# A three-stage transformer block on one core: its planner gets one place per step, a rule for products and reads that share a double PSUM tile, longer v loads and fillers of 256 columns

## The chip, the cores and the metric

The kernel runs on one core of a Trainium2 chip. The metric is the device time of one execution in microseconds (us). Three runs of the kernel before gave 773.05, 774.28 and 776.44 us; their median, 774.28 us, is the time that is compared.

## The reference

Everything is computed from float32 attention inputs and 64-bit weights:

```python
# attention: q, k, v are (4, 8, 576, 64); heads 0-3 a plain window of 32, heads 4-7 a dilated one (32 keys, step 4)
scores = scale * np.matmul(q, k.transpose(0, 1, 3, 2))
scores = np.where(masks[None, :, :, :], scores, -1000000000.0)
attn = np.exp(scores - max); attn = attn / (sum + 1e-09)
x = np.matmul(attn, v)                            # then (2304, 512)
# gated layer: w_gate, w_val (512, 1536), w_out (1536, 512)
x = (silu(x @ w_gate) * (x @ w_val)) @ w_out
# second layer: w_in (512, 1024), w_out (1024, 512), g_ln (1024)
h = x @ w_in
solu = h * softmax(h)
out = (solu - mean) / np.sqrt(var + 1e-06) * g_ln @ w_out
```

## The kernel before, in words

All large products run in float16 with every operand split into a high and a low part, so that each product is three matmuls (`PASSES`, line 65: high by high, high by low, low by high). The weights come as 64-bit numbers; they are converted on the chip by integer and float operations on ScalarE (ACT), VectorE (DVE) and GpSimd (POOL) (`w_conv`, `w_scale`, `w_split`, lines 598 to 797), and q, k, v, the attention output x, the gated product u and y are split in the same way (`split`, line 512: a high part, then a low part of the difference).

The work goes through 4 batches and 12 blocks of 192 tokens. For each batch, four pairs of heads go through `prep_T` (line 993, q and k transposed by TensorE (PE) for batches 0 and 1, by DMA for 2 and 3), `s1` (1108, scores and exponentials), `s2` (1216, the turned probabilities) and `s3` (1262, product with v and the split of x, lines 1307 to 1313). For each block, six chunks of `a_chunk` (1318) give the gated product: 48 matmuls at line 1339, then a Silu on ACT at line 1351 and the gate on DVE at line 1360, here called gate 1, gate 2 and so on in their order on DVE. Then come `b_part` (1413, product with w_out at line 1423, result y, split into `yhl`), and for each 128 tokens `c_part`, `c_exp`, `c_post` (1460 to 1555, product at line 1471 and the softmax and normalisation), `z_T` (1561) and `d_part` (1589, the last product at line 1599 and the store).

PSUM is held in five tiles (line 297): `ps0`, `ps1`, `ps2` are double (two banks of 512 columns each), `ps3` is single, `ps4` holds sums in its first half and receives the fillers. Results of kind 2 (A chunks, scores, turned tiles, h) take a whole double tile. Results of kind 1 (x in `s3`, y in `b_part`, the output in `d_part`; line 313) take `ps3` or one half of a double tile.

The order of all of this is not that of the code. Each piece of work is a step with an engine, an assumed cost, and the data that it reads and writes (`Plan.step`, line 95). `Plan.schedule` (157) then goes through a modelled time and takes, of the steps that could start soonest on an engine, the one with the smallest `urg`. Before, `urg` is the TensorE time planned so far less a lead and less a number of its own for each part of the work (the table `sl` in `OPT`, line 61). The order that comes out is what every engine's queue executes; the real waits are semaphores, which keep the data right whatever the plan assumed. While the planned PE would wait, the plan inserts fillers (line 302, matmuls of a 128 by 128 tile of ones into the unused part of `ps4`), each planned at `FILL` (line 79), only for planned times below 320 us (`OPT["fill"]`), and with no waiting of their own in the plan. Loads go out from the SyncE queue (SP), except that two of the first four v loads are issued from ACT's queue (`vact`, line 55; `load`, line 835).

Of the kernel before, what the change touches and what calls it, by code (L numbers as in the profile page):

```python
# [27 lines left out]
    "alap": 0.0,  # L28
# [26 lines left out]
    "vact": [0, 0, 1, 1],  # L55
# [11 lines left out]

class Bank:


    def __init__(self, of, kind):
        self.of, self.kind, self.at, self.users = of, kind, None, 0

    def get(self):
        return self.of(self.at)

FILL = 128 / 2400 + 0.0027


class Plan:

    PIPE = {"ACT": 0.1, "DVE": 0.09, "PE": 0.16, "POOL": 0.05, "SP": 0.0}
    LAT = 0.05

    def __init__(self):
# [3 lines left out]
    def step(self, eng, cost, fn, r=(), w=(), lat=0.0, tab=None, dense=1.0, starts=1, port=False):  # L95
        deps = {}
        for k in r:
            if k in self.writer:
                d = self.writer[k]
                deps[d["n"]] = d  # L100
        for k in w:
            for d in self.readers.get(k, ()):
                deps[d["n"]] = d
            if k in self.writer:
                d = self.writer[k]
                deps[d["n"]] = d
        st = {"n": len(self.steps), "eng": eng, "cost": cost, "fn": fn, "deps": list(deps.values()), "lat": lat,
              "tab": tab, "dense": dense, "starts": starts, "port": port or eng == "POOL", "end": None, "left": len(deps), "outs": [], "part": self.part, "urg": self.urgency - self.lead - OPT["sl"].get(self.part, 0.0), "ready": 0.0}
        for d in st["deps"]:
            d["outs"].append(st)  # L110
        for k in w:
            self.writer[k], self.readers[k] = st, []
        for k in r:
            self.readers.setdefault(k, []).append(st)
        st["banks"] = {k for k in list(r) + list(w) if isinstance(k, Bank)}
        for k in st["banks"]:
            k.users += 1
        if eng == "PE":
            self.urgency += cost
        self.steps.append(st)  # L120
# [19 lines left out]
    def lags(self, t):  # L140
# [3 lines left out]
        return self.busy < OPT["keep"] * (into + 3.413) - 0.3  # L144

    def rank(self):

        f = OPT["alap"]
        for st in reversed(self.steps):
            late = st["urg"] + st["cost"] if st["eng"] == "PE" or not st["outs"] else 1e9  # L150
            for o in st["outs"]:
                late = min(late, o["rank"] - (self.LAT + st["lat"]) * f)
            st["rank"] = late - st["cost"] * (1.0 if st["eng"] == "PE" else f)
        for st in self.steps:
            st["urg"] = st["rank"]

    def schedule(self):
        if OPT["alap"]:
            self.rank()
        free, tab = {"SP": 1.9, "ACT": 1.9, "DVE": 0.6, "POOL": 0.6}, "exp"  # L160
        self.busy, self.warm, self.window = 0.0, False, 0
        ready = [st for st in self.steps if not st["left"]]

        bank_free, order, issued, done = [0.0] * 8, [], 0.6, []
        held = {"DVE": [], "POOL": []}
        choices = {2: [(0, 1), (2, 3), (4, 5)], 1: [(6,), (0,), (1,), (2,), (3,), (4,), (5,)], "sum": [(7,)]}
        no = float("inf")

        def places(kind):

            for at in choices[kind]:
                broken = 0 if kind != 1 or at[0] == 6 else bank_free[at[0] ^ 1] != no
                yield max(bank_free[x] for x in at), broken, at

        while ready:
            cand, soonest = [], {kind: min(places(kind))[0] for kind in choices}
            for st in ready:
                t = max(free.get(st["eng"], 0.0), st["ready"])
                if st["port"]:
                    for a, b in held["POOL" if st["eng"] == "DVE" else "DVE"]:  # L180
                        if a <= t < b:
                            t = b
                for k in st["banks"]:
                    if k.at is None:
                        t = max(t, soonest[k.kind])
                if t == no:
                    continue

                on = st["eng"] == "POOL" and st["ready"] <= free["POOL"] == t
                cand.append((t, not on, st["urg"], st["n"], st))  # L190
# [65 lines left out]
def kernel(  # L256
# [13 lines left out]
    nc = tc.nc  # L270
# [29 lines left out]
    def idle(n):  # L300
        for _ in range(n):
            nc.tensor.matmul(out=ps_t[4][:, 0, 256:384], lhsT=ones, rhs=ones, start=True, stop=True)  # L302
# [1584 lines left out]
```

## Time and profile before

| | |
|---|---|
| median of three runs | 774.28 us |
| the profiled execution: its own time | 775.11 us |
| the profiled execution: its span | 773.3 us |
| PE busy | 742.7 us, 96% of the span |
| DVE, ACT, POOL busy | 510.3, 474.7, 233.0 us |
| fillers | 781 matmuls, 52.4 us busy |
| mean granted PE clock | 0.993 of full speed |

The span runs from the first to the last instruction that the profiler saw; the execution's own time holds 1.8 us more, around the span. A busy time is the union of an engine's instructions. The clock is the share of 2.4 GHz that was granted to PE, so that 0.5 is its lower level, 1.2 GHz.

### The profile page before, as it was taken

What the parts mean: (1) busy time and instruction counts of PE and PEld (TensorE: products, weight loads), DVE (VectorE), ACT (ScalarE), POOL (GpSimd) and SP (SyncE); (2) the same over time, 40 slices, a digit from 0 to 9 for tenths busy, and PEclk for the clock granted to TensorE, in tenths of its full rate; (3) what the DMA queues carried; (4) which work ended last, traced back from release to release, by engine and by line L of the source; (5) the groups of instructions that cost most, each with busy time, mean ns of one, the idle gap of its engine ahead of it and who ended that gap; (6) DMA issues with size and microseconds to landing.
All of it is one profiled execution on the core that took longest, in us unless ns stands there. A gap on an engine that the chain in (4) does not pass through costs nothing.

```text
span 773.3 us, 19396 instructions
## 1 busy us (share of the span) xinstructions
PE 742.7 (96%) x8044; PEld 622.2 (80%) x8044; DVE 510.3 (66%) x1059; ACT 474.7 (61%) x1020; POOL 233.0 (30%) x188
## 2 busy tenths in 40 slices
PE   6998999989999999999999999989999999999998
PEld 6888989889996888668865889968867889897754
DVE  3688988988987969778795557556665133116653
ACT  2878988976665767878762457656744344426432
POOL 1445145574663233142452124423420000110000
PEclk9999999999999999999999999999999999999999
DMA  8885933423435242645845371434222101001101
GB/s 205 212 260 180 247 125 109 112 72 110 148 70 160 60 113 50 131 106 90 144 105 112 76 118 20 77 79 77 44 45 44 26 15 29 14 3 21 35 14 55
DMA packets 149816, 71.79 MB, mean 93 GB/s; under 512 B 136032, under 2 KB 136032, under 8 KB 149216
## 3 DMA queue, kind: packets, MB, share of 16 engines
q1 hardware_dynamic: 146688, 69.80, 37.2%
q8 instruction: 63, 1.03, 0.6%
q10 hardware_dynamic: 3040, 0.75, 0.6%
q14 instruction: 25, 0.20, 0.1%
HBM read 46.14 MB, written 4.72 MB: 66 GB/s over the span
## 4 chain that ended last, share of the span: by engine, by line
PE 78%; DVE 10%; ACT 7%; DMA 3%; SPq 2%; issue 1%; ACTq 0%; DVEq 0%
PE ps L1339 28%; PE ps L1423 18%; PE ps L1471 12%; PE ps L1599 12%; PE ps L302 3%; PE ps L1152 2%; ACT sm L1193 1%; DMA area<-in_moe_w_gate_dram 1%; PE ps L1280 1%; SPq L857 1%; DVE sml L1174 1%; PE ps L1237 1%; PE ps L1275 1%; SPq L838 1%; DVE area L641 1%
## 5 line engine op out<-in xcount | busy, mean ns | idle before, releaser
L1339 PE MATMUL ps<-x,gv 128*128 128x192 f16 x3456 | 296.6, 247 | 3.3 <-DVE area L1360 2.3
L1339 PEld LDWEIGHTS <-gv 128*128 128x128 f16 x3456 | 286.7, 98 | 10.9 <-issue 5.3
L1423 PE MATMUL ps<-uhl,area 128*128 128x192 f16 x1728 | 150.1, 246 | 2.8 <-DVE x L531 1.9
L1423 PEld LDWEIGHTS <-area 128*128 128x128 f16 x1728 | 142.3, 98 | 6.0 <-issue 3.3
L1471 PE MATMUL ps<-area,yhl 128*128 128x512 f16 x432 | 98.7, 381 | 0.0
L1599 PE MATMUL ps<-area 128*128 128x512 f16 x408 | 94.0, 383 | 3.0 <-DVE yhl L531 3.0
L1360 DVE SCALAR_TENSOR_TENSOR u<-ps,c_gv,si 128x384 f32<-128x384 f32 x60 | 36.4, 611 | 77.2 <-ACT si L1351 77.2
L1212 POOL TENSOR_TENSOR sm<-sm,sml 96x768 f32<-96x768 f32 x28 | 46.5, 1662 | 118.4 <-DVE sml L1208 76.0
L1471 PEld LDWEIGHTS <-yhl 128*128 128x128 f16 x432 | 41.2, 98 | 46.2 <-issue 1.1
L1599 PEld LDWEIGHTS <-area 128*128 128x128 f16 x408 | 39.2, 98 | 47.4 <-issue 4.4
L1351 ACT ACTIVATE si<-ps,c_gv 128x384 f32<-128x384 f32 x72 | 41.4, 578 | 46.9 <-PE ps L1339 42.2
L1531 POOL TENSOR_TENSOR sml<-sml,nhalf 128x2 f32<-128x2 f32 x18 | 13.4, 743 | 167.3 <-DVE sml L1528 161.0
L302 PE MATMUL ps<-ones 128*128 128x128 bf16 x781 | 52.4, 226 | 5.6 <-DVE wsc L485 3.8
L302 PEld LDWEIGHTS <-ones 128*128 128x128 bf16 x781 | 48.3, 102 | 6.8 <-issue 4.5
L611 POOL TENSOR_TENSOR area<-area 128x512 int32<-128x512 int32 x28 | 38.4, 1388 | 47.4 <-ACT area L624 22.3
L1366 ACT ACTIVATE si<-u 128x384 f32<-128x384 f32 x60 | 31.2, 521 | 25.2 <-DVE u L1360 24.9
L543 POOL TENSOR_TENSOR qk<-qk,qk 96x768 f16<-96x768 f32 x16 | 27.8, 1735 | 47.0 <-DVE qk L522 25.7
L1193 ACT ACTIVATE sm<-sm,sml 96x128 f32<-96x128 f32 x96 | 37.2, 388 | 4.2 <-DVE sml L1187 3.9
L1496 ACT ACTIVATE area<-ps,sml 128x1024 f32<-128x1024 f32 x18 | 21.7, 1204 | 25.3 <-DVE sml L1491 25.1
L1551 ACT ACTIVATE area<-area,sml 128x1024 f32<-128x1024 f32 x17 | 21.0, 1237 | 22.8 <-DVE sml L1545 22.8
L1351 ACT ACT_TABLE_LOAD x24 | 30.8, 1283 | 4.6 <-PE ps L1339 4.2
L1490 DVE TENSOR_REDUCE sml<-ps 128x1 f32<-128x1024 f32 x18 | 21.9, 1218 | 17.5 <-PE ps L1471 15.5
(226 smaller groups left out, 1143.5 us busy)
## 6 DMA issues: line engine op xcount, KB each, us to landing
area<-in_moe_w_out_dram SPq DMA_DIRECT2D x10, 1024.0 KB, 4.9
area<-in_moe_w_gate_dram SPq DMA_DIRECT2D x6, 1024.0 KB, 7.5
area<-in_moe_w_val_dram SPq DMA_DIRECT2D x6, 1024.0 KB, 7.3
out_dram<-area SPq DMA_DIRECT2D x18, 256.0 KB, 2.0
area<-in_moe_w_in_dram SPq DMA_DIRECT2D x4, 1024.0 KB, 5.3
qk<-in_v_dram SPq DMA_DIRECT2D x9, 384.0 KB, 4.3
qk<-in_q_dram SPq DMA_DIRECT2D x20, 144.0 KB, 3.5
qk<-in_k_dram SPq DMA_DIRECT2D x18, 144.0 KB, 3.4
```

The costliest lines, as they stand in the source:

```text
L302: nc.tensor.matmul(out=ps_t[4][:, 0, 256:384], lhsT=ones, rhs=ones, start=True, stop=True)
L543: step("POOL", n / 480 + 0.05, lambda: nc.gpsimd.tensor_tensor(out=lo(), in0=src(), in1=hi(), op=ALU.subtract), r=list(sk) + list(hk), w=lk)
L611: step("POOL", 1.23, lambda: nc.gpsimd.tensor_tensor(out=ti[:, x], in0=ti[:, x], in1=part[:, x], op=ALU.add), r=rk, w=tk)
L1193: nc.scalar.activation(out=smv[:, n], in_=view()[0:QB, n // 3, n % 3] if on_pe else smv[:, n], func=ACTF.Exp, bias=nm[:, n:n + 1], scale=c ...
L1212: step("DVE" if OPT["pn"][b] else "POOL", dve(768) if OPT["pn"][b] else 1.43, lambda: on.tensor_tensor(out=smv, in0=smv, in1=rs.unsqueeze( ...
L1339: nc.tensor.matmul(out=view()[:, ff, w], lhsT=wt[:, a, kk, (f % 4) * 128:(f % 4) * 128 + 128], rhs=x[:, c, kk, BLK * o:BLK * o + BLK], sta ...
L1351: step("ACT", act(384) + 0.06, lambda: nc.scalar.activation(out=si, in_=view()[:, :, 0], func=ACTF.Silu, scale=c_gv[:, b, 2 * ci:2 * ci + 1]),
L1360: nc.vector.scalar_tensor_tensor(out=uu, in0=view()[:, :, 1], scalar=c_gv[:, b, 2 * ci + 1:2 * ci + 2], in1=si, op0=ALU.mult, op1=ALU.mult)
L1366: step("ACT", act(384) + 0.1, lambda: nc.scalar.activation(out=si.rearrange("p f t -> p (f t)"), in_=uu.rearrange("p f t -> p (f t)"), fun ...
L1423: nc.tensor.matmul(out=bk.get()[:, 0, cc * BLK:cc * BLK + BLK], lhsT=whl[6 + f // 4][:, a, f % 4, c * 128:(c + 1) * 128], rhs=uhl[:, e, f] ...
L1471: nc.tensor.matmul(out=bk.get()[:, half], lhsT=yhl[:, i, c, o:o + 128], rhs=w_in_hl[m][:, e, c % 2, half * 512:half * 512 + 512], start=(c ...
L1599: nc.tensor.matmul(out=bk.get()[:, 0], lhsT=zt[:, c, kk], rhs=whl[11 + half][:, e, kk % 4], start=(kk == 0 and n == 0), stop=(kk == 7 and ...
```

## The change

Five things change. The table `sl` and the function `rank` go; a list `PRI` holds one number for each step of the program, and `schedule` puts it into `urg`. The planner keeps for each bank when its neighbour in the double tile was last read and written (`beside`): a planned PE write of kind 1 doesn't start before the end of the reads of the other half, and a planned read not before the end of the writes to the other half. Assumed costs are raised: v loads to 2.5 or 3.9 us (from 2.05), `cgv`, `u_scale`, the plain `prep_T` copy and the split of x by 0.05 to 0.26 us. No v load is issued from ACT any more. A filler has 256 columns, on the same 128 weights. No other instruction's work is changed; a place in PSUM, and where a tile load or activation table falls, follows from the order.

```diff
-    "alap": 0.0,
-    "vact": [0, 0, 1, 1],
+    "vact": [0, 0, 0, 0],
-    "sl": {"A0.0": 705.2, "A0.1": 389.6,
...
+PRI = [
...
-FILL = 128 / 2400 + 0.0027
+FILL = 256 / 2400 + 0.0027
...
     def schedule(self):
-        if OPT["alap"]:
-            self.rank()
+        assert len(PRI) == len(self.steps)
+        for st, at in zip(self.steps, PRI):
+            st["urg"] = at
...
+        beside = {"read": [0.0] * 8, "written": [0.0] * 8}
...
-                yield max(bank_free[x] for x in at), broken, at
+                yield max([bank_free[x] for x in at] + ([beside["read"][at[0] ^ 1]] if kind == 1 and at[0] < 6 else [])), broken, at
...
                     if k.at is None:
                         t = max(t, soonest[k.kind])
+                    elif len(k.at) == 1 and k.at[0] < 6:
+                        t = max(t, beside["read" if st["eng"] == "PE" else "written"][k.at[0] ^ 1])
...
+                seen = beside["written" if st["eng"] == "PE" else "read"]
+                for x in k.at:
+                    seen[x] = max(seen[x], st["end"] + self.PIPE[st["eng"]] + self.LAT)
...
-            nc.tensor.matmul(out=ps_t[4][:, 0, 256:384], lhsT=ones, rhs=ones, start=True, stop=True)
+            nc.tensor.matmul(out=ps_t[4][:, 0, 256:512], lhsT=ones, rhs=ones.unsqueeze(1).to_broadcast([128, 2, 128]), start=True, stop=True)
...
-        step("DVE", 0.14, fn, r=[("wsc", 2 * c), ("wsc", 2 * c + 1), ("vsc", b)], w=[("cgv", b, c)])
+        step("DVE", 0.23, fn, r=[("wsc", 2 * c), ("wsc", 2 * c + 1), ("vsc", b)], w=[("cgv", b, c)])
...
-        load(2.05, fns, key, act=b == 0 and OPT["vact"][O0.index(pr)])
+        load(2.5 if dil else 3.9, fns, key, act=b == 0 and OPT["vact"][O0.index(pr)])
```

The program's lines move down by 90 from line 157 on: line 302 before is line 392 now, line 1360 is 1450. Counted over the whole program, the fillers go from 781 to 299, the loads of an activation table on ACT from 49 to 39, and everything else that PE, DVE and POOL execute stays in kind and number. Three places show how the order moves.

The head of SP's queue, which issues the loads (in a row: what is written, what is read, and x2 for two alike). Before:

```order
L595 DMA area_72<-in_moe_w_gate_dram 128x4x256
L838 DMA v32_1_91<-in_v_dram 96x2x64
...
L838 DMA v32_1_91<-in_v_dram 128x2x64
L838 DMA qk0_92<-in_q_dram 96x6x64 x2
L838 DMA uhl_109<-in_k_dram 96x6x64 x2
L595 DMA area_72<-in_moe_w_val_dram 128x4x256
L838 DMA yhl_110<-in_v_dram 96x2x64
```

And now:

```order
L928 DMA uhl_109<-in_k_dram 96x6x64 x2
L928 DMA qk0_92<-in_q_dram 96x6x64 x2
L685 DMA area_72<-in_moe_w_gate_dram 128x4x256
L928 DMA qk1_93<-in_q_dram 96x6x64 x2
L928 DMA v32_1_91<-in_v_dram 96x2x64
...
L928 DMA v32_1_91<-in_v_dram 128x2x64
L685 DMA area_72<-in_moe_w_val_dram 128x4x256 x2
L928 DMA v32_0_90<-in_v_dram 96x2x64
```

The first k and q stood behind half a gate matrix and eight pieces of v; they now stand first, and both halves of the value matrix follow in one go.

The start of POOL's queue, which makes the constants: `ones` is what the fillers multiply. Before:

```order
L1619 MEMSET ident_73 128x128
L1620 ISA
L1620 AFFINE_SELECT ident_73<-ident_73 128x128
L1625 MEMSET ones_76 128x128
L1626 MEMSET nhalf_77 128x1
L1627 MEMSET eps_78 1x1
L1627 MEMSET one32_79 128x1
L1637 CAST id16_75<-ident_73 96x96
L1639 MEMSET mask_74 96x640
L1640 AFFINE_SELECT mask_74<-mask_74 96x640
L1643 AFFINE_SELECT mask_74<-mask_74 96x640
```

And now:

```order
L1710 AFFINE_SELECT ident_73<-ident_73 128x128
L1093 MEMSET gv2_68 128x32
L1727 CAST id16_75<-ident_73 96x96
L1729 MEMSET mask_74 96x640
L1730 AFFINE_SELECT mask_74<-mask_74 96x640
L1733 AFFINE_SELECT mask_74<-mask_74 96x640
L1737 MEMSET mask_74 96x32
L1739 AFFINE_SELECT mask_74<-mask_74 96x80
L1093 MEMSET kT1_98 128x32
L1715 MEMSET ones_76 128x128
```

`ones` has moved behind the mask. PE's queue begins with fillers in both: 125 before the first transpose (line 1043) then, 19 now.

DVE's queue in the third batch, where x is split out of half of a double tile (`x0<-ps2`) while y is read from, and written into, the other half. Before:

```order
L522 TENSOR_SCALAR x0_103<-ps2_63 128x2x144
L531 SCALAR_TENSOR_TENSOR x0_103<-ps2_63,x0_103 128x2x144
L531 SCALAR_TENSOR_TENSOR yhl_110<-ps2_63,rel_85,yhl_110 128x2x192
L531 SCALAR_TENSOR_TENSOR area_72<-area_72,rel_85 128x512
L522 TENSOR_SCALAR x0_103<-ps2_63 128x2x144
L509 TENSOR_REDUCE sml_111<-qk1_93 96x1
L531 SCALAR_TENSOR_TENSOR x0_103<-ps2_63,x0_103 128x2x144
```

And now:

```order
L612 TENSOR_SCALAR x0_103<-ps0_61 128x2x144
L621 SCALAR_TENSOR_TENSOR yhl_110<-ps0_61,rel_85,yhl_110 128x2x192
L621 SCALAR_TENSOR_TENSOR x0_103<-ps0_61,x0_103 128x2x144
...
L1580 TENSOR_REDUCE sml_111<-ps2_63 128x1
L1581 TENSOR_SCALAR sml_111<-sml_111 128x1
L612 TENSOR_SCALAR x0_103<-ps0_61 128x2x144
L621 SCALAR_TENSOR_TENSOR x0_103<-ps0_61,x0_103 128x2x144
```

Tiles are still shared by x and y, but on another tile and with other work between; over the program 1,152 of the 1,728 matmuls of line 1423 now write into half of a double tile, against 792 before.

## Rows read from the trace of the kernel before

**Rows 1.** The page, part 1: busy time, share of the span, instructions.

```profile
PE 742.7 (96%) x8044; PEld 622.2 (80%) x8044; DVE 510.3 (66%) x1059; ACT 474.7 (61%) x1020; POOL 233.0 (30%) x188
```

**Rows 2.** Windows: stretch, length, busy PE, PEld, DVE, ACT, POOL; PE clock, DMA share, GB/s.

```profile
0.00:23.50 23.50, 17.08 (x223) 16.36 (x224) 9.53 (x18) 7.42 (x19) 3.95 (x21) 0.93 0.75 186
23.50:84.97 61.47, 56.53 (x876) 52.20 (x875) 50.25 (x98) 53.91 (x148) 29.67 (x21) 1.00 0.79 231
84.97:175.79 90.82, 85.12 (x1041) 81.84 (x1038) 79.40 (x151) 79.06 (x172) 46.21 (x32) 0.98 0.41 120
175.79:221.20 45.41, 43.63 (x572) 41.51 (x571) 40.52 (x91) 27.58 (x72) 25.32 (x20) 1.00 0.44 127
221.20:773.30 552.10, 540.33 (x5346) 430.25 (x5343) 330.59 (x708) 306.73 (x614) 127.84 (x95) 1.00 0.32 66
```

**Rows 3.** The same windows for the fillers (line 302) alone.

```profile
0.00:23.50 23.50, 13.18 (x174) 12.86 (x175) 0.93 0.75 186
23.50:84.97 61.47, 32.18 (x511) 29.46 (x508) 1.00 0.79 231
84.97:175.79 90.82, 2.94 (x41) 2.40 (x41) 0.98 0.41 120
175.79:221.20 45.41, 4.11 (x59) 3.60 (x59) 1.00 0.44 127
```

**Rows 4.** Waits of PE: waiting line, releaser: us in total, times, longest.

```profile
PE ps L1599 <- DVE yhl L531: 3.0, 1, 3.0
PE ps L1339 <- DVE area L1360: 2.3, 1, 2.3
...
PE ps L1423 <- DVE x L531: 1.9, 2, 1.0
...
PE ps L1423 <- DVE x L522: 0.9, 1, 0.9
```

**Rows 5.** Timeline of PE at the start: start, length, what [idle before, releaser].

```profile
1.51 9.11 PE L302 MATMUL ps<-ones 128*128 128x128 bf16 x125 [1.51 <-POOL ones L1625]
15.26 0.72 PE L1043 MATMUL ps<-ident,qk 96*128 96x96 f32 x6 [4.63 <-DMA qk<-in_q_dram]
...
22.63 2.51 PE L302 MATMUL ps<-ones 128*128 128x128 bf16 x42
```

**Rows 6.** Timeline of POOL at the start: the last constant.

```profile
4.45 0.18 POOL L1003 MEMSET gv<- 128x32 f32 x2
```

**Rows 7.** Timeline of SP at the start: the first v load, and the value matrix.

```profile
1.27 9.71 SPq L838 DMA_DIRECT2D v<-in_v_dram  x8
...
13.80 0.63 SPq L595 DMA_DIRECT2D area<-in_moe_w_val_dram  x1
```

**Rows 8.** Timeline of DVE: gates 18 and 19; gate 1 starts at 84.97 us.

```profile
175.79 0.60 DVE L1360 SCALAR_TENSOR_TENSOR area<-ps,c_gv,si 128x384 f32<-128x384 f32 x1
...
221.20 0.61 DVE L1360 SCALAR_TENSOR_TENSOR u<-ps,c_gv,si 128x384 f32<-128x384 f32 x1
```

**Rows 9.** A group of DVE: mean ns of one stands ahead of the last bar.

```profile
L641 DVE SCALAR_TENSOR_TENSOR area<-area 128x1024 int32<-128x1024 int32 x17 | 23.6, 1390 | 5.9 <-POOL area L611 5.9
```

**Rows 10.** Timeline of PE, around two waits at shared tiles.

```profile
412.89 1.64 PE L1423 MATMUL ps<-uhl,area 128*128 128x192 f16 x18 [0.89 <-DVE x L522]
...
513.31 1.46 PE L1599 MATMUL ps<-area 128*128 128x512 f16 x6
517.82 2.72 PE L1599 MATMUL ps<-area 128*128 128x512 f16 x6 [3.05 <-DVE yhl L531]
```

**Rows 11.** Timeline of DVE at the same two places.

```profile
412.04 0.80 DVE L522 TENSOR_SCALAR x<-ps 128x288 f16<-128x288 f32 x1 [0.56 <-PE ps L1423]
...
517.16 0.60 DVE L531 SCALAR_TENSOR_TENSOR yhl<-ps,rel,yhl 128x384 f16<-128x384 f32 x1
```

**Rows 12.** Windows, all engines, after two of PE's longest waits.

```profile
170.00:174.00 4.00, 4.00 (x34) 3.85 (x32) 3.24 (x7) 3.97 (x14) 1.00 (x1) 0.64 0.00 0
...
516.00:520.00 4.00, 2.19 (x6) 0.79 (x6) 3.93 (x10) 2.45 (x5) 0.00 (x0) 0.71 0.40 74
```

More of the change, by code (lines that the diff above doesn't have):

```diff
@@ L62 @@
 }
+PRI = [
[91 rows of a table added]
+]
 PASSES = ((0, 0), (0, 1), (1, 0))
@@ L107, in step @@
         st = {"n": len(self.steps), "eng": eng, "cost": cost, "fn": fn, "deps": list(deps.values()), "lat": lat,
-              "tab": tab, "dense": dense, "starts": starts, "port": port or eng == "POOL", "end": None, "left": len(deps), "outs": [], "part": self.part, "urg": self.urgency - self.lead - OPT["sl"].get(self.part, 0.0), "ready": 0.0}
+              "tab": tab, "dense": dense, "starts": starts, "port": port or eng == "POOL", "end": None, "left": len(deps), "outs": [], "part": self.part, "urg": self.urgency - self.lead, "ready": 0.0}
         for d in st["deps"]:
@@ L144, in lags @@
         return self.busy < OPT["keep"] * (into + 3.413) - 0.3
[L146 to L155, printed above, removed]
     def schedule(self):
-        if OPT["alap"]:
-            self.rank()
+        assert len(PRI) == len(self.steps)
+        for st, at in zip(self.steps, PRI):
+            st["urg"] = at
         free, tab = {"SP": 1.9, "ACT": 1.9, "DVE": 0.6, "POOL": 0.6}, "exp"
@@ L1086, in prep_T @@
             return
-        step("ACT", act(S) + (0.29 if len(parts) == 1 else 0.42), hi, r=[bk] + sk + dk, w=hk)
+        step("ACT", act(S) + (0.55 if len(parts) == 1 else 0.42), hi, r=[bk] + sk + dk, w=hk)
         step("DVE", dve(S) + 0.1 * len(parts), lo, r=[bk] + sk + hk, w=dk)
@@ L1308, in s3 @@
             split(288, lambda: dst[0], hk, lambda: dst[1], x_key(b, pr, g), src, xk, 1.0, (), OPT["xpl"][b],
-                  more=0.3 if pr >= 2 else 0.0)
+                  more=0.4 if pr >= 2 else 0.1)
             return
@@ L1312, in s3 @@
               *((vsc[:, b, 2], [("vsc", b)]) if PV[b] == "f" else (2.0 ** -10, ())), way=OPT["xpl"][b], psum=True,
-              more=0.3 if pr >= 2 else 0.0)
+              more=0.35 if pr >= 2 else 0.08)
     uam = {}
@@ L1392, in fn @@
                     out=t[:, n:n + 1], in0=rel[:, n:n + 1], scalar1=usc[:, j, 2], scalar2=None, op0=ALU.mult)
-        step("DVE", 0.2, fn, r=[("rel", 0), ("usc", j)], w=tk)
+        step("DVE", 0.34, fn, r=[("rel", 0), ("usc", j)], w=tk)
     def u_split(j):
```

1 line of the change is left out of this document (removed), and 91 rows, old and new, of the table PRI.

## The prediction

> **What bounds the kernel now.** I read the page's busy times first: PE is busy 742.7 of 773.3 us [rows 1], so nothing but its fillers and its idle time can go. The windows cut the span at gates 1, 18 and 19, where DVE hands the first, eighteenth and nineteenth gated chunk on [rows 2, 8]; the same windows for the fillers alone [rows 3] are to be taken off PE's busy time. What is left is PE's real work, and the length of a stretch less its real work is what PE wastes there:
>
> - 0 to 23.5 us: 23.5 − (17.08 − 13.18) = 19.6
> - to 84.97: 61.47 − (56.53 − 32.18) = 37.1
> - to 175.79: 90.82 − (85.12 − 2.94) = 8.6
> - to 221.20: 45.41 − (43.63 − 4.11) = 5.9
> - to the end: 552.1 − 540.33 = 11.8
>
> In all 83.0 us: 52.4 of fillers and 30.6 idle; the real work is 690.3 us. So two thirds of what can be won lies ahead of gate 1. But PE doesn't set the time there: from 23.5 to 84.97 us DVE is busy 50.25 and ACT 53.91 of 61.47 us, and from there to gate 18 both some 79 of 90.8 us, while the DMA engines work at 186 and 231 GB/s in the first two stretches [rows 2]. The converted weights and the split x come from DVE and ACT; a filler only sits in that wait. After gate 19, PE works at 98%, and DVE at 60%.
>
> **The change part by part.** *Fillers.* 482 of 781 go, and the rest are twice as wide. A warm one of 128 columns takes 2.51/42 = 59.8 ns [rows 5]; with twice that at most, 299 take 35.8 us against 52.4, which is 16.6 us less. This is what PE would save if the waits shrank as the fillers do and its idle time stayed. It is no price: where the data come late, the missing filler is idle time instead. I take it as the far end.
>
> *The start.* PE's first transpose waited for q until 15.26 us, 4.63 of it idle [rows 5], since q stood behind a v load whose eight pieces took SP 9.71 us [rows 7]. Now k and q go first. Against that, `ones` moves behind the mask on POOL: it was ready at 1.51 us, when the fillers began [rows 5], and the work that now precedes it ended at 4.45 + 0.18 = 4.63 us [rows 6]. The plan starts its fillers at 1.5 us and knows no such wait, but this is what held PE in the trace [rows 5]. Its queue begins with 19 fillers; each costs 0.12 us, or 0.24 at half the clock (the first 125 took 9.11 us instead of 125 × 59.8 ns = 7.5, so the clock was low at first), so 2.3 to 4.6 us. The first transpose comes at 6.9 to 9.2 us, 6 to 8 earlier than before. On the path this gives less: the value matrix went out at 13.80 us behind gate, v, q and k [rows 7], and now stands behind gate, two q, k and the same eight pieces of v, so at about the same time. The first stretch of DVE is mostly waiting for those (9.53 busy of 23.5). I price it at nothing, between 0 and −6.
>
> *The order up to gate 18.* Ahead of gate 18, DVE's queue holds 257 instructions before and 255 now, of the same kinds, and ACT's 4 table loads less. So the change can only take DVE's idle time there: 61.47 − 50.25 = 11.2 us from 23.5 to 84.97, and 90.82 − 79.40 = 11.4 to gate 18 [rows 2]. Longer assumed costs and a place for each step should order some of that away; steps that arrive later than assumed will still stop a fixed queue. Nothing in the trace prices it: the ends are 0 and two thirds, 15.1 us (DVE then idles 5%, less than in any stretch now). I take one third, **−7.5 us**, nearer to the end that the trace shows.
>
> *Shared double tiles.* At 517.82 us PE stopped 3.05 us in the middle of a product of line 1599, whose first six matmuls had run at 513.31 without a wait; what released it was DVE's read of y at 517.16, from the other half of the same tile [rows 10, 11]. At 412.89 PE waited 0.89 us for the split of x, which itself waited 0.56 us for PE [rows 10, 11]: the two take turns. With the waits of line 1423 on x this is 3.0 + 1.9 + 0.9 = 5.8 us [rows 4]. The wait of 3.05 us also cost clock: the six matmuls after it took 2.72 us instead of 1.46 [rows 10], and the granted clock was 0.71 in that window [rows 12]; 1.3 us more. Ends: 0 (the tiles are still shared, by more matmuls than before) and −7.1. The planner now sees these waits and puts other products between, so I take **−4.5 us**. The Trainium skill, page PSUM — Partial Sum Buffer, section PSUM bank collisions raise a hardware error, says that only accesses to the same bank and quadrant must be kept apart, and that different banks run clean together. By that rule the halves, two banks, need no waiting, and a planner that keeps them apart gains nothing: the sum would be 4.5 us higher. The row shows PE stopped all the same, so the wait is one that the program asks for, and I go by the row.
>
> *The rest.* The raised costs of `cgv`, `u_scale`, `prep_T` and the split add no instruction. The v loads leave ACT's queue for SP's: six issues more there, at a time when the DMA engines are 75% busy anyway [rows 2]. Ten table loads less free ACT, which waits more than it works after gate 18 (27.58 of 45.41 us).
>
> **Sum.** −7.5 − 4.5 = −12.0 us on the profiled execution, whose own time is 775.11 us, 1.8 over its span. Its time is 0.83 above the median, 774.28; from there −12 gives 762.
>
> **The rivals.**
>
> *PE's own waits shrink as its fillers do.* Fillers −16.6, shared tiles −7.1, together −23.7, so 751; with a little of the start as well, 748. For it: the plan sees more of the real costs, and its order is free at each step. Against: DVE must then idle less than 5% up to gate 18.
>
> *Nothing moves where it counts.* DVE idles as before up to gate 18, and new waits take the place of those at shared tiles: 773.
>
> *DVE becomes later: slower.* Ahead of gate 19, DVE's queue holds 359 instructions now against 346: four splits of y at 0.60 us and nine conversions or splits, the longest at 1.39 us [rows 9, 11], some 12 us more, while PE's real work ahead of that chunk is the same. From 23.5 us to gate 19 DVE was busy 50.25 + 79.40 + 40.52 = 170.2 of 197.7 us, 86% [rows 2, 8]. At 86% the 182 us now needed end at 23.5 + 212 = 235 us, 14 later than 221.20. PE can work some 5 us ahead (estimate: two thirds of the 7.4 us between its chunk and the gate), so 9 us are lost; 2 of the 4.5 at shared tiles come back: 781. It decides at 92% (182 of 197.7): DVE that full or fuller, and gate 19 isn't late. The work that was brought forward is then missing behind, where DVE has room, which speaks against it.
>
> *The clock falls more often.* After waits of 2.3 and 3.05 us [rows 4, 10] the granted clock was 0.64 and 0.71 over 4 us [rows 12]. With 482 fillers fewer, more waits are bare; six of them at some 1.5 us each would take 9 of the 12: 771. The Trainium skill, TensorE: Matmul & The Clock Gate, section HAM oscillation — how this bites in real kernels, says that a DMA wait in each round sends PE back to the low clock every time. The trace shows it for the two longest waits; but in the first 85 us PE's speed isn't what counts, so I give it little.
>
> **How the numbers follow.** A measurement of this kernel tells 0.5% (3.9 us) from no change. The forecast, 754 to 770, has 0.53; PE's waits shrinking 0.20; nothing moves 0.13; DVE later 0.08; the clock 0.06. Faster than 770.4 are the first two, and of the clock and of nothing moving about a third: 0.79. Slower than 778.2 is the DVE case, 0.07; 0.14 is left within. The range takes in the far end of the fillers and the case without a gain: 746 to 776. The likeliest case's own range is 754 to 770.
>
> **What would show it.** PE's first transpose at 7 to 9 us, and its first filler held until about 4.6 us by POOL. The fillers at 30 to 36 us. Gate 18 at 166 to 170 us, with DVE busy about 88 to 90% from 23.5 us on. No wait of line 1599 or 1423 for a split over 1 us. ACT's table loads 10 fewer. Wrong, if gate 18 stays at 175 us, if gate 19 comes after 225, or if PE's idle time beyond 221 us is no less than 11.8.

## The result, and the profile after

The changed kernel takes 763.18 us (median of 761.93, 763.13, 763.24 and 763.59), the kernel before in the same series 773.66. The ratio is 0.986, with a 95% interval from 0.983 to 0.989: 10.5 us, 1.4% faster. The profiled execution took 763.24 us, its span 761.5; that is 11.8 us less than the span before.

The products with the weights stand at lines 1429, 1513, 1561 and 1689 now (1339, 1423, 1471 and 1599 before).

Part 1 of the page after, as [rows 1]:

```profile
PE 732.4 (96%) x7562; PEld 605.2 (79%) x7562; DVE 511.5 (67%) x1059; ACT 460.2 (60%) x1010; POOL 236.1 (31%) x188
```

The windows after, cut at gates 1, 18 and 19 as in [rows 2] (stretch, length, busy PE, PEld, DVE, ACT, POOL; PE clock, DMA share, GB/s):

```profile
0.00:23.50 23.50, 13.65 (x98) 10.55 (x99) 9.96 (x24) 12.08 (x42) 6.68 (x23) 0.87 0.83 213
23.50:87.02 63.52, 59.83 (x668) 51.04 (x667) 54.99 (x106) 53.88 (x143) 30.12 (x21) 0.99 0.81 232
87.02:164.14 77.12, 74.09 (x896) 71.53 (x894) 70.77 (x134) 64.52 (x134) 40.95 (x31) 0.98 0.42 125
164.14:221.32 57.18, 55.40 (x681) 52.22 (x680) 56.36 (x105) 38.49 (x94) 35.55 (x24) 1.00 0.40 119
221.32:761.50 540.18, 529.44 (x5229) 419.91 (x5226) 319.46 (x695) 291.27 (x599) 122.84 (x93) 1.00 0.32 66
```

The same windows after for the fillers alone, as [rows 3]:

```profile
0.00:23.50 23.50, 8.87 (x43) 5.85 (x43) 0.87 0.83 213
23.50:87.02 63.52, 28.37 (x220) 20.52 (x218) 0.99 0.81 232
87.02:164.14 77.12, 1.08 (x7) 0.61 (x7) 0.98 0.42 125
164.14:221.32 57.18, 4.37 (x31) 2.83 (x31) 1.00 0.40 119
```

What PE wastes in a stretch is its length less PE's real work (PE's busy time less its fillers):

| stretch | before | after | difference |
|---|---|---|---|
| start to gate 1 | 19.6 + 37.1 = 56.7 | 18.7 + 32.1 = 50.8 | −5.9 |
| gate 1 to 18 | 8.6 | 4.1 | −4.5 |
| gate 18 to 19 | 5.9 | 6.2 | +0.3 |
| gate 19 to the end | 11.8 | 10.7 | −1.1 |
| all | 83.0 | 71.8 | −11.2 |

The other 0.6 us is real work, 689.7 us against 690.3. So 10.4 of the 11.8 us were won ahead of gate 18, which both kernels reach with nearly the same real work of PE done (110.4 us before, 109.3 after). Gate 18 starts at 164.14 us, 11.65 earlier; gate 19 at 221.32, where it was. That takes nothing back: PE came to gate 19 with about 10 us more of its work done (202.97 − 42.69 = 160.3 us of real work by then, 202.36 − 52.41 = 150.0 before). A gate's time alone doesn't show a lead; PE's real work up to it does.

Behind gate 19 the small net hides two large terms. The windows there hold no fillers in either kernel. Before:

```profile
221.00:260.00 39.00, 39.00 (x383) 32.22 (x381) 31.51 (x53) 27.73 (x45) 13.59 (x9) 1.00 0.42 119
260.00:300.00 40.00, 40.00 (x429) 35.16 (x427) 31.74 (x73) 26.73 (x46) 11.84 (x9) 1.00 0.28 68
300.00:600.00 300.00, 292.03 (x2999) 230.57 (x2997) 201.45 (x431) 185.16 (x409) 93.39 (x68) 0.99 0.44 84
```

After:

```profile
221.00:260.00 39.00, 35.16 (x344) 28.89 (x342) 27.46 (x50) 23.45 (x39) 16.85 (x11) 1.00 0.49 122
260.00:300.00 40.00, 39.64 (x369) 30.96 (x369) 32.68 (x79) 28.54 (x59) 10.46 (x8) 1.00 0.23 54
300.00:600.00 300.00, 297.32 (x3134) 240.49 (x3132) 195.89 (x419) 176.67 (x401) 86.86 (x65) 1.00 0.42 82
```

From 300 to 600 us PE wins 5.3 us: there lay the waits at shared tiles of [rows 4], 5.8 us of them, and they are gone. (The 1.1 us that line 1429 waits for x in the list below are no such wait: its products read x.) From 221 to 300 us it loses 4.2, in waits that weren't there. PE's longest waits after:

```profile
PE ps L392 <- DVE wsc L575: 6.9, 5, 4.7
PE ps L392 <- POOL ones L1715: 4.6, 1, 4.6
PE ps L1242 <- DVE area L1450: 2.1, 1, 2.1
PE ps L1561 <- DVE u L1450: 1.8, 1, 1.8
PE ps L1429 <- DVE u L1450: 1.3, 1, 1.3
PE ps L1429 <- DVE x L621: 1.1, 2, 0.8
```

Of [rows 4], the waits of lines 1599 (now 1689) and 1423 (now 1513) for a split have no successor in this list. The 1.3 and the 1.8 us are for gates 20 and 22; 0.8 of the rest is for line 1595. The chain behind the two gates reads off ACT's timeline and then DVE's:

```profile
224.65 0.84 ACT L616 ACTIVATE qk<-qk 96x768 f16<-96x768 f32 x1 [2.02 <-POOL qk L633]
225.40 0.56 ACT L1441 ACTIVATE si<-ps,c_gv 128x384 f32<-128x384 f32 x1
...
231.81 1.14 ACT L711 ACTIVATE area<-area 128x1024 f32<-128x1024 f32 x1 [1.96 <-DMA area<-in_moe_w_out_dram]
232.85 1.13 ACT L714 ACTIVATE area<-area 128x1024 int32<-128x1024 uint32 x1
233.87 0.58 ACT L1441 ACTIVATE si<-ps,c_gv 128x384 f32<-128x384 f32 x1
```

```profile
225.99 0.62 DVE L1450 SCALAR_TENSOR_TENSOR u<-ps,c_gv,si 128x384 f32<-128x384 f32 x1 [2.88 <-ACT si L1441]
...
234.48 0.62 DVE L1450 SCALAR_TENSOR_TENSOR u<-ps,c_gv,si 128x384 f32<-128x384 f32 x1 [0.80 <-ACT si L1441]
```

The Silu of gate 20 stands on ACT behind a split of q or k that waits 2.02 us for POOL. The Silu of gate 22 stands behind two conversions of w_out, and the first of these waits 1.96 us for its load. At both gates DVE waits for the Silu, and PE for DVE.

The start after, on PE's timeline, as [rows 5]:

```profile
4.64 4.24 PE L392 MATMUL ps<-ones 128*128 128x256 bf16 x19 [4.64 <-POOL ones L1715]
8.66 1.17 PE L1133 MATMUL ps<-ident,uhl 96*128 96x96 f32 x6
```

### The profile page after: what moved, and what is told of

The parts are those of the page before. It is cut to its first block, busy times and chain, and to the rows that moved or that the text cites. A ratio compares the mean times of both kernels' runs of the same rounds, so it can differ in the third digit from the quotient of the medians.

```text
span 761.5 us, 18448 instructions
## 1 busy us (share of the span) xinstructions
PE 732.4 (96%) x7562; PEld 605.2 (79%) x7562; DVE 511.5 (67%) x1059; ACT 460.2 (60%) x1010; POOL 236.1 (31%) x188
## 4 chain that ended last, share of the span: by engine, by line
PE 56%; DVE 21%; ACT 11%; issue 6%; POOL 4%; DMA 2%; SPq 0%; POOLq 0%; ACTq 0%; DVEq 0%
PE ps L1429 21%; PE ps L1513 11%; PE ps L1561 9%; PE ps L1689 9%; ACT sm L1283 3%; PE ps L392 2%; PE ps L1242 1%; DVE x L621 1%; DMA out_dram<-area 1%; DVE sml L1264 1%; DVE sml L1580 1%; POOL qk L633 1%; ACT L1283 1%; DVE sml L1607 1%; DVE area L1595 1%
## 5 line engine op out<-in xcount | busy, mean ns | idle before, releaser
L1302 POOL TENSOR_TENSOR sm<-sm,sml 96x768 f32<-96x768 f32 x28 | 44.1, 1574 | 123.0 <-DVE sml L1298 90.4
L392 PE MATMUL ps<-ones 128*128 128x256 bf16 x299 | 42.7, 290 | 11.9 <-DVE wsc L575 6.9
L701 POOL TENSOR_TENSOR area<-area 128x512 int32<-128x512 int32 x28 | 40.7, 1466 | 33.1 <-ACT area L714 11.6
L633 POOL TENSOR_TENSOR qk<-qk,qk 96x768 f16<-96x768 f32 x16 | 29.7, 1857 | 57.9 <-DVE sml L1078 20.1
L392 PEld LDWEIGHTS <-ones 128*128 128x128 bf16 x299 | 29.8, 103 | 18.0 <-issue 8.1
L1283 ACT ACTIVATE sm<-sm,sml 96x128 f32<-96x128 f32 x96 | 37.2, 388 | 10.8 <-DVE sml L1277 10.6
L616 ACT ACTIVATE yhl<-ps,rel 128x384 f16<-128x384 f32 x24 | 13.3, 576 | 43.4 <-PE ps L1513 26.1
L633 POOL TENSOR_TENSOR uhl<-u,uhl 128x768 f16<-128x768 f32 x12 | 19.5, 1643 | 52.5 <-ACT uhl L616 52.5
L621 DVE SCALAR_TENSOR_TENSOR area<-area,rel 128x512 f16<-128x512 f32 x30 | 24.6, 829 | 13.6 <-ACT area L616 10.6
```

The lines of the kernel that those rows point to most:

```text
L392: nc.tensor.matmul(out=ps_t[4][:, 0, 256:512], lhsT=ones, rhs=ones.unsqueeze(1).to_broadcast([128, 2, 128]), start=True, stop=True)
L621: step("DVE", dve(n) + by + more, lambda: nc.vector.scalar_tensor_tensor(out=lo(), in0=src(), scalar=scale, in1=hi(), op0=ALU.mult, op1=AL ...
L633: step("POOL", n / 480 + 0.05, lambda: nc.gpsimd.tensor_tensor(out=lo(), in0=src(), in1=hi(), op=ALU.subtract), r=list(sk) + list(hk), w=lk)
L701: step("POOL", 1.23, lambda: nc.gpsimd.tensor_tensor(out=ti[:, x], in0=ti[:, x], in1=part[:, x], op=ALU.add), r=rk, w=tk)
L1283: nc.scalar.activation(out=smv[:, n], in_=view()[0:QB, n // 3, n % 3] if on_pe else smv[:, n], func=ACTF.Exp, bias=nm[:, n:n + 1], scale=c ...
L1302: step("DVE" if OPT["pn"][b] else "POOL", dve(768) if OPT["pn"][b] else 1.43, lambda: on.tensor_tensor(out=smv, in0=smv, in1=rs.unsqueeze( ...
```

## The experiments

Each ratio is to runs of the kernel before on the same chip, with its 95% interval. The gates are from DVE's timeline of the profiled execution; three executions whose order up to there is the same (after, e1, e9) had gate 1 at 87.02, 86.30 and 87.53, so a microsecond at a gate says little.

| kernel | median us | ratio | gate 1 | gate 18 | gate 19 | gate 41 | last gate |
|---|---|---|---|---|---|---|---|
| before | 773.66 | 1 | 84.97 | 175.79 | 221.20 | 457.21 | 707.30 |
| e1 control | 762.67 | 0.986 (0.983 to 0.988) | 86.30 | 163.28 | 220.47 | 450.51 | 697.37 |
| e2 ones first | 762.27 | 0.985 (0.983 to 0.987) | 85.17 | 162.62 | 219.80 | 450.35 | 697.09 |
| e3 no fillers | 765.55 | 0.990 (0.988 to 0.992) | 88.28 | 165.58 | 222.71 | 452.89 | 700.32 |
| e4 narrow fillers | 760.29 | 0.982 (0.980 to 0.984) | 84.49 | 161.23 | 218.37 | 449.04 | 695.95 |
| e5 no rule | 768.89 | 0.992 (0.989 to 0.995) | 88.77 | 164.85 | 222.40 | 453.93 | 703.39 |
| e6 before, rule | 790.80 | 1.022 (1.018 to 1.025) | 85.53 | 179.09 | 229.71 | 468.70 | 722.92 |
| e7 old priorities | 847.66 | 1.094 (1.090 to 1.099) | 95.45 | 161.19 | 235.56 | 503.16 | 774.70 |
| e8 before, places | 775.97 | 1.001 (0.999 to 1.003) | 87.26 | 165.10 | 224.05 | 460.30 | 710.86 |
| e9 moved | 763.11 | 0.985 (0.982 to 0.987) | 87.53 | 164.72 | 220.33 | 452.98 | 699.86 |
| e10 combined | 760.08 | 0.982 (0.979 to 0.985) | 84.28 | 161.65 | 217.24 | 448.83 | 695.72 |
| e11 planned narrow | 762.25 | 0.983 (0.981 to 0.986) | 84.85 | 161.88 | 218.91 | 448.12 | 694.70 |
| e12 v price undone | 760.09 | 0.983 (0.981 to 0.985) | 87.04 | 163.62 | 218.47 | 447.68 | 694.57 |

### e1: the control

No edit.

> The changed kernel once more, unaltered, as the yardstick for the three beside it: 762 to 764 us, ratio 0.985 to 0.988, by either theory.

762.67 us, ratio 0.986, as expected.

### e2: ones first

```diff
-        step("POOL", 0.1, lambda: nc.gpsimd.memset(ones, 1.0), w=[("ones",)])
+        step("POOL", 0.1, lambda: nc.gpsimd.memset(ones, 1.0), w=[("ones",)])
+        P.steps[-1]["first"] = True
...
+            if st.get("first"):
+                st["urg"] = -1
```

> The changed kernel with the matrix of ones made first on POOL; nothing else in the order moves. Both theories: the first filler is held until about 1.5 us instead of 4.64, and the first transpose comes at 5 to 6 us instead of 8.66. Theory A (the start is bound by the loads of q, k and the gate matrix and by what DVE and ACT do with them, so I priced the start at nothing): the second stretch takes it back, time within 1 us of the control. Theory B (PE's start sets the first gates, through ACT's copies of the transposes): gate 1 comes 3 us earlier, 84 instead of 87, and the time falls by 2 to 3 us.

PE's timeline at the start:

```profile
0.99 4.24 PE L394 MATMUL ps<-ones 128*128 128x256 bf16 x19 [0.99 <-POOL ones L1717]
5.02 1.17 PE L1135 MATMUL ps<-ident,uhl 96*128 96x96 f32 x6
```

The first transpose comes 3.65 us earlier. Gate 1 comes 1.1 us earlier, about the spread, gate 41 0.2, and the time falls by 0.4. Theory A holds: PE's late start costs no more than about that, which is less than the spread of the four runs (761.94 to 763.46). e10 shows where the next wait lies: there the transpose waited 1.6 us for the load of k and began at 4.82 us.

### e3 and e4: without fillers, and with narrow ones

```diff
     def idle(n):
         for _ in range(n):
-            nc.tensor.matmul(out=ps_t[4][:, 0, 256:512], lhsT=ones, rhs=ones.unsqueeze(1).to_broadcast([128, 2, 128]), start=True, stop=True)
+            pass
```

for e3, and for e4 the matmul of before in its place, with `256:384` and `rhs=ones`. The plan still counts with 256 columns.

> The changed kernel with its plan and order as they are, but none of the 299 fillers issued. Theory A (the fillers only sit in waits for DVE, ACT and loads, and their one use is to hold the granted clock): PE's idle time rises by about the 42.7 us they took, the granted clock to gate 1 falls clearly below 0.9, and the time is between that of the control and 5 us above it. Theory B (PE's queue is late because of the fillers, so fewer of them are the gain): 2 us or more faster than the control, gate 1 at 85 us or earlier.

> The changed kernel with the same 299 fillers in the same places, each 128 columns wide as before instead of 256. Theory A: the time they no longer take becomes idle time, fillers 18 to 26 us, idle up by as much as they fall; time within 1 us of the control unless the clock falls in more windows, then up to 3 us above. Theory B (the width of the fillers delays the products behind them): 2 us or more faster than the control.

Part 1 of the page, of the control, e3 and e4 in turn, and then the fillers' groups of the control and of e4:

```profile
PE 731.4 (96%) x7562; PEld 604.3 (79%) x7562; DVE 510.3 (67%) x1059; ACT 460.0 (60%) x1010; POOL 236.5 (31%) x188
```

```profile
PE 715.2 (94%) x7263; PEld 590.9 (77%) x7263; DVE 511.4 (67%) x1059; ACT 460.7 (60%) x1010; POOL 236.1 (31%) x188
```

```profile
PE 719.2 (95%) x7562; PEld 597.3 (79%) x7562; DVE 508.6 (67%) x1059; ACT 459.7 (61%) x1010; POOL 238.7 (31%) x188
```

```profile
L392 PE MATMUL ps<-ones 128*128 128x256 bf16 x299 | 42.4, 289 | 11.9 <-DVE wsc L575 6.9 <-POOL ones L1715 4.6 <-DVE vsc L571 0.2
```

```profile
L392 PE MATMUL ps<-ones 128*128 128x128 bf16 x299 | 26.5, 240 | 11.9 <-DVE wsc L575 6.8 <-POOL ones L1715 4.6 <-DVE vsc L571 0.2
```

The spans are 760.6, 763.6 and 759.2 us. What each kernel's PE did more or less than the control's (its busy time less fillers is its other work):

| | fillers | idle | other work of PE | span |
|---|---|---|---|---|
| e3 | −42.4 | 48.4 − 29.2 = +19.2 | 715.2 − 689.0 = +26.2 | +3.0 |
| e4 | 26.5 − 42.4 = −15.9 | 40.0 − 29.2 = +10.8 | 692.7 − 689.0 = +3.7 | −1.4 |

Theory A is right about e3's time: without fillers the kernel is 2.9 us slower. It isn't right about the rest. Idle time rose by 19.2 us, not by 42.7; more of the fillers' time turned into slower work. And the granted clock up to gate 1, foretold below 0.9, stands at 1.00 in this execution (the last section says why). The same twelve matmuls at the start, in the control and in e3:

```profile
11.57 0.90 PE L1242 MATMUL ps<-kT,qT 64*96 64x128 f32 x12 [0.58 <-ACT qT L1157]
```

```profile
9.20 1.59 PE L1242 MATMUL ps<-kT,qT 64*96 64x128 f32 x12 [1.05 <-ACT qT L1157]
```

23 of the 26 us lie ahead of gate 1, where the same 506 matmuls took 58.8 us instead of 35.6. They cost only 3 us of time, since PE isn't what sets the time there. e4 went as theory B has it: it is 2.4 us faster than the control, and none of its four runs (758.6 to 760.95) reaches the control's (762.4 to 763.72). Its first transpose came at 6.64 us instead of 8.67, gate 1 1.8 us and gate 18 2.1 us earlier. So 299 wide fillers delay the products behind them, by about 2 us in all, against 299 narrow ones; having the wide ones rather than none is worth about 3. Whether it is the width or the sum of their time (15.9 us less) is the question of e11.

### e5: without the rule on double tiles

```diff
-                seen = beside["written" if st["eng"] == "PE" else "read"]
-                for x in k.at:
-                    seen[x] = max(seen[x], st["end"] + self.PIPE[st["eng"]] + self.LAT)
```

> The changed kernel, its planner without the rule on the two halves of a double PSUM tile; priorities, costs and fillers as they are. Its order leaves that of the changed kernel after some 600 rows of PE's queue. Theory A (the rule takes away PE's waits for a read of the other half, some 5 us between 300 and 600 us): waits of the SolU lines 1429, 1513 and 1561 (numbers of the changed kernel) for a split of x, u or y return, 3 to 6 us of them, and the time is 766 to 769 us. Theory B (such waits only take the place of others, and the gain is all made ahead of gate 18): the time stays within 1.5 us of the control, 761 to 764 us.

768.89 us: theory A. Of PE's waits (lines 3 lower here), these are for splits:

```profile
PE ps L1510 <- DVE yhl L618: 1.3, 1, 1.3
PE ps L1686 <- DVE x L618: 1.0, 1, 1.0
PE ps L1426 <- DVE x L618: 1.0, 2, 0.6
...
PE ps L1686 <- ACT yhl L613: 0.7, 1, 0.7
```

The first answers to the expectation's line 1513, the third to 1429, and line 1689, which it didn't name, has 1.7. The products of line 1429 read x, and the control waits there too (0.8 us). The products of the other three, and of line 1370 (0.3 us for y), don't read what the split writes for which they wait: that makes 3.3 us at shared tiles, where the control's list has none. Against the control, the kernel is 2.5 us behind at gate 1, 1.9 at gate 19, 3.4 at gate 41 and 6.0 at the last: some 4 us of the loss lie behind gate 19. The rest was there at gate 1 already: PE's order differs from 67 us on, and a microsecond at a gate is spread. The medians are 6.2 us apart, the ratios 0.006 (4.8 us).

### e6, e7 and e8: rule and places apart

e6 is the kernel before with the rule's lines alone, and each step's priority its place in the order of before:

```diff
-        order = self.schedule()
+        order = self.schedule(False)
+        for n, st in enumerate(order):
+            st["urg"] = n
...
+        order = self.schedule(True)
```

> The kernel before with that rule alone: its own order is worked out first, each step's place in it becomes the step's priority, and the order is then worked out again with the rule. Theory A: the 3.0 us wait of line 1599 and the 2.8 us of line 1423 for splits (numbers of the kernel before) go, and the time falls by 4 to 6 us, to 768 to 770 us. Theory B: other waits take their place, 773 to 776 us.

790.80 us. Of the waits of lines 1599 and 1423 for splits 0.4 us are left, as theory A said, but the time rose by 16 us, which neither theory had: the order holds 953 fillers of 63.2 us, and new waits stand in it (for `et` by DMA 4.9 us, for `sml` 3.4). PE's order differs from that of before from some 52 us on, and what comes out is an order that nobody fitted.

e7 is the changed kernel with the priorities of before:

```diff
-        assert len(PRI) == len(self.steps)
-        for st, at in zip(self.steps, PRI):
-            st["urg"] = at
...
-"urg": self.urgency - self.lead, "ready": 0.0}
+"urg": self.urgency - self.lead - OPT["sl"].get(self.part, 0.0), "ready": 0.0}
```

> The changed kernel with the rule, the costs and the wide fillers, but each step's priority as in the kernel before (by urgency and the shift of its part). Theory A (the step's own places make the gain ahead of gate 18, the rule that behind 300 us): gate 18 comes at 172 to 178 us instead of 164, the shared-tile waits stay away, and the time is 768 to 771 us. Theory B (the rule and the raised costs make the gain, the places only write them down): 762 to 766 us, gate 18 at 163 to 168. An order that nobody has fitted can also come out worse than either, above 774 us; then it tells only what an unfitted order costs.

847.66 us: the last case of the expectation. The old priorities were fitted under the old rule and prices; under the new ones they make an order 11% slower than the control. It tells nothing of the two theories, but it shows what a gate's time is worth. Its gate 18 came at 161.19 us, 14.6 earlier than before, yet PE had done only 153.32 − 58.40 = 94.9 us of real work by then (110.4 before); 58.40 us were fillers. Its window up to gate 18:

```profile
0.00:161.19 161.19, 153.32 (x1699) 140.57 (x1700) 120.89 (x226) 108.71 (x251) 62.35 (x64) 1.00 0.57 170
```

e8 is the kernel before with the places and the v loads on SP:

```diff
-    "vact": [0, 0, 1, 1],
+    "vact": [0, 0, 0, 0],
...
-        if OPT["alap"]:
-            self.rank()
+        assert len(PRI) == len(self.steps)
+        for st, at in zip(self.steps, PRI):
+            st["urg"] = at
```

> The kernel before with the places as priorities and the v loads on SP, but without the rule, with the old costs and with fillers of 128 columns. Theory A: gate 18 comes at 162 to 168 us as in the changed kernel, waits for the other half of a double tile remain, 3 to 6 us, and the time is 766 to 769 us. Theory B (without the rule and the costs the places aren't worth anything): 772 us or more.

Gate 18 came at 165.10 us and 4.3 us of waits at shared tiles remain, as theory A has it; the time is that of the kernel before, as theory B has it. Its windows, cut at gates 18 and 19, in all and then for the fillers alone:

```profile
0.00:165.10 165.10, 146.06 (x1902) 138.03 (x1903) 136.63 (x262) 131.01 (x318) 81.29 (x73) 0.97 0.61 178
165.10:224.05 58.95, 55.75 (x736) 53.22 (x735) 52.44 (x106) 38.78 (x94) 34.12 (x24) 1.00 0.40 116
224.05:300.00 75.95, 72.99 (x744) 60.48 (x743) 53.66 (x110) 47.07 (x83) 25.78 (x18) 1.00 0.33 86
```

```profile
0.00:165.10 165.10, 37.16 (x512) 33.74 (x512) 0.97 0.61 178
165.10:224.05 58.95, 7.85 (x123) 7.19 (x123) 1.00 0.40 116
224.05:300.00 75.95, 4.79 (x77) 4.46 (x77) 1.00 0.33 86
```

Up to gate 18 PE wastes 165.10 − (146.06 − 37.16) = 56.2 us, 9.1 less than before: the places with the v loads on SP bring nearly the whole lead of the changed kernel (10.4). But from gate 18 to 19 this kernel wastes 11.1 us (5.9 before, 6.2 in the changed kernel), and from there to 300 us 7.8 (0 and 4.2), 12.6 of these 18.8 us in fillers, which the plan put there because it saw PE waiting. DVE is busy 52.44 of 58.95 us between the two gates, where the changed kernel has 56.36 of 57.18. So the lead was real and was lost behind gate 18, in the plan's own order. Which of the missing parts (the rule, the raised costs, the wide fillers in the plan) would have kept it isn't settled; e12 says that the price of v alone isn't needed.

### e9 and e10: small steps behind gate 22, and the three together

```diff
         order = self.schedule()
+        late = [st for st in order if st["n"] in (710, 723, 828, 856, 891, 894, 892, 893, 899)]
+        order = [st for st in order if st not in late]
+        at = [st["n"] for st in order].index(703) + 1
+        order[at:at] = late
```

> The changed kernel with nine small steps of DVE that are needed late (the scales of u and of the gated chunks and one of q and k, 14 instructions that took 1.9 us between 209.8 and 221.3 us) moved behind gate 22; nothing else moves. Theory A (between gates 18 and 19 DVE is full, and its extra work there is what took back the 11.6 us by which gate 18 came earlier): gate 19 comes 1.5 to 2 us earlier than in the control, at 218.5 to 219, and PE's idle time from there to 260 us falls from 4.2 us by about as much; time 0.5 to 2 us below the control. Theory B (gates 20 to 22 wait for PE's products and ACT's silu, not for DVE's queue): gate 19 is earlier, gates 20 to 22 and the time are not, within 0.5 us.

From gate 18 to 19 it took 55.6 us instead of 57.2, as both theories had it. The time stayed (763.11 against 762.67), as theory B has it; its reason holds for gate 22 alone. Gates 20 and 21 came earlier by the same 1.6 us, counted from gate 18, and PE's wait of 1.3 us for gate 20 is gone. But gate 22 came 69.95 us after gate 18 instead of 70.45, and PE then waited 2.8 us for it instead of 1.9. First ACT's timeline ahead of that gate, then the window behind PE's wait in e9 and the same one in the control (columns as in the windows above):

```profile
232.00 1.14 ACT L715 ACTIVATE area<-area 128x1024 f32<-128x1024 f32 x1 [3.14 <-DMA area<-in_moe_w_out_dram]
...
234.05 0.58 ACT L1445 ACTIVATE si<-ps,c_gv 128x384 f32<-128x384 f32 x1
```

```profile
236.00:240.00 4.00, 4.00 (x25) 3.47 (x24) 3.17 (x12) 1.55 (x4) 0.77 (x1) 0.58 0.42 91
236.00:240.00 4.00, 4.00 (x34) 2.76 (x32) 2.03 (x2) 2.73 (x7) 0.00 (x0) 1.00 0.48 99
```

ACT waited 3.14 us for the load of w_out with the Silu of gate 22 behind it, and after the longer wait PE's granted clock fell to 0.58 in the next 4 us, where it was 1.00 in the control. That the load is the cause is read from this row; a kernel in which the Silu goes ahead of the conversions wasn't tried.

e10 adds the edits of e2 and e4 to this one.

> The same move, the matrix of ones first on POOL, and fillers of 128 columns in the places of the wide ones. If the three are independent, the control less 2.4 (narrow), less 0.4 (ones) and less what the move alone gives: 758 to 760 us, first transpose at about 3.5 us, gate 1 at 83.5 to 84.5. If the narrow fillers and the ones win the same wait at the start: 760 to 761.

760.08 us, just over the sum's range and no less than e4 alone (760.29), as the second case has it. But the six runs go from 758.10 to 765.10, and gate 1 came at 84.28 us, within the sum's range, so the two cases aren't told apart. The first transpose came at 4.82 us, not 3.5, held by the load of k. By their medians, both e4 and e10 beat the changed kernel by 2 to 3 us; the interval of e10 overlaps with the control's.

### e11: narrow fillers in the plan too

```diff
-FILL = 256 / 2400 + 0.0027
+FILL = 128 / 2400 + 0.0027
```

with the matmul of e4.

> The changed kernel with fillers of 128 columns in the plan as well, so that some 570 of them fill the same planned waits; the order of everything else is unchanged. Theory A (what the products behind a filler lose is the time by which the fillers in the queue outlast the real wait, and each filler costs more than the plan thinks): 570 narrow ones fill as much as 299 wide ones, so the time is within 1 us of the control, 762 to 764. Theory B (wide fillers as such are slower): 760 to 761 as with 299 narrow ones.

569 fillers took 40.7 us, nearly what 299 wide ones take, and the median of 762.25 is theory A's. But the four runs spread from 759.71 to 762.76, and the interval holds the ratio of the control as well as that of e4: not settled.

### e12: the price of the v loads undone

```diff
-        load(2.5 if dil else 3.9, fns, key, act=b == 0 and OPT["vact"][O0.index(pr)])
+        load(2.05, fns, key, act=b == 0 and OPT["vact"][O0.index(pr)])
```

> The changed kernel with the planned price of a v load back at 2.05 us; rule, places, fillers and the other prices as they are. The order changes from the first v load on (PE's from its row 186). Theory A (every price is part of the order for which the places were found, and the v loads' price sets when DVE and PE take the steps behind them): 764 to 770 us, more waits for v or for what comes of it before gate 1. Theory B (the v price is nothing beside the rule and the places): 762 to 764.

760.09 us: theory A falls, and the time lies below the range of theory B too. The new price brings nothing here; by the medians the kernel is 2.6 us faster without it, by the ratios 0.003, with intervals that overlap. Gate 18 stands where it was, and from 221.3 to 260 us PE is busy 37.5 of 38.7 us (34.4 in the control): that order lacks the waits at gates 20 and 22 (0.3 us of them left). It wastes as much elsewhere: in all 757.8 − (731.5 − 45.3) = 71.6 us, the control's figure; what is smaller in the profiled execution is PE's other work, 686.2 us against 689.0.

## Why the prediction was right

It gave 762.0 us (754 to 770 for the forecast case); the time is 763.18. The sign and the two mechanisms were right, and both show in the runs. That the sum came so close is partly luck: the order up to gate 18 gave 2.9 us more than its term and the shared tiles 0.8 more, and a term that was missing took 4.2 back.

- **The order up to gate 18**, −7.5: the table of waste shows −10.4, and gate 18 came at 164.14 us, ahead of the foretold 166 to 170. The third of DVE's idle time was the right share: from 23.5 us to gate 18 it fell from 22.6 to 14.9 us, by 7.8. What was wrong is that the change could take nothing else. DVE's busy time there fell too, from 50.25 + 79.40 = 129.7 to 54.99 + 70.77 = 125.8 us, and 7.8 + 3.9 is the whole 11.65 us by which the gate came earlier. One line alone (1206, now 1296) changes by 3.8, while the others nearly cancel: 13 small instructions were busy 5.7 us before, with up to 1.19 us for one, and 11 of them 2.0 after, at most 0.37. Why some took so long before stays open. DVE was busy 125.8 of 140.6 us, 89%, within the foretold 88 to 90%. e8 shows that the places, with the v loads on SP, bring 9.1 of the 10.4 us; those two were not taken apart.
- **Shared tiles**, −4.5: 5.3 us in the windows from 300 to 600 us, and about 4 us behind gate 19 by e5. No wait of lines 1689 and 1513 for a split is left in the list, as foretold, and PE's idle time behind gate 19 is 540.18 − 529.44 = 10.7 us, under the 11.8 of before. The row on which I went against the rule of the Trainium skill (page PSUM — Partial Sum Buffer, section PSUM bank collisions raise a hardware error) held: it says that different banks run clean together, yet without the planner's rule PE waits 3.3 us at shared tiles (e5), and with it the list shows no such wait. Whether two separate tiles instead of one double tile would need no such wait wasn't tried.
- **The missing term**: +4.2 us of new waits from 221 to 300 us. The prediction named no successor at gates 20 to 22 for the stalls that go. What is late there is a Silu on ACT: gate 20's behind a split that waits for POOL, gate 22's behind a conversion that waits for w_out. The two cost PE 1.3 and 1.8 us of the 4.2. That these waits are the cause is read from the trace; e12, whose other order lacks both, agrees.
- **DVE later ahead of gate 19** was counted rightly and decided as stated: DVE was busy 54.99 + 70.77 + 56.36 = 182.1 of 197.8 us up to gate 19, the 182 us and the 92% at which I had put the deciding point, and gate 19 came at 221.32, no later than before.
- **The fillers**: 42.7 us, not 30 to 36. The bound of 119.6 ns was for the higher clock. The first 19 took 4.24 us, 223 ns each, which is nearly twice that, as at the lower clock; the 43 in the first 23.5 us took 206 ns each, the other 256 on average 132. That their time isn't a price was right in kind, but not to the end: e4 shows that narrow ones in the same places win 2.4 us.
- **The start**, 0: first transpose at 8.66 us, first filler held until 4.64 by POOL, both as foretold. e2 gives 0.4 us for the late ones; what q and k at the head of SP's queue bring was not tried alone.
- **The v loads**: their planned price brings nothing by e12, rather a small loss. Their move to SP's queue, priced at nothing, was not tried alone.
- **The clock** as a rival didn't decide: PE's real work took 689.7 us, 690.3 before. The mean granted clock is 0.993 in both kernels, but it leaves out the low clock at the start (last section). After that, the changed kernel has one fall, 0.78 and 0.79 over 104 to 112 us behind a wait of 2.1 us, where the kernel before has two [rows 12]. ACT has 10 instructions fewer, the table loads that were foretold [rows 1].

## What to carry to other kernels

When a list scheduler fits an order, its rules, prices and priorities belong together: the rule alone made the kernel 16 us slower, the old priorities under the new rule and prices 85 us slower than the control, the places without rule and prices gave nothing, and together they gave 10.5. Not every part is needed: the price of the v loads could go without loss (e12). So undo parts to see what each holds, but don't read the sum off single parts; and where the rule or the priorities change, fit again. Measure a lead by the bottleneck engine's real work done, not by the time of one milestone: gate 18 came 14.6 us early in e7, the slowest of these kernels, and gate 19 not at all early in one that gained 11. And follow a lead to the end, since e8 had 9 us of it at gate 18 and lost it all.

## What the runs showed that I had not expected

Without fillers PE's matmuls ran at about half speed for most of the time ahead of gate 1, while the column of the granted clock stood at 1.00 in these windows of e3. The same form of twelve matmuls that took 1.59 us at 9.20 us, and still 1.60 at 64.17, took this later in the same execution:

```profile
76.79 0.90 PE L1242 MATMUL ps<-kT,qT 64*96 64x128 f32 x12 [0.19 <-ACT kT L1157]
```

The first clock record in e3's trace is a rise at 70.3 us (at 5.7 us in the kernel before, 10.7 in the changed one), and the column counts what lies ahead of the first record as 1.00. So it shows the falls of a clock that had risen, not a clock that hasn't risen yet; a matmul's own duration shows both. For the same reason the mean clocks of executions don't compare: 0.995 in this one of e3, 0.962 to 0.972 in the five others, at about the same time. And a wait of 2.8 us was followed by a granted clock of 0.58 where one of 1.9 us was followed by 1.00, at the same place of two nearly equal orders.
